# A fused layernorm, Fourier filter and MLP kernel: the program's block is taken away, and one small early read with it

## The chip, the cores and the metric

The kernel runs on one core of one Trainium2 chip. The core has five engines that run their own instruction streams: TensorE (PE in the profile; its weight loads are listed as PEld), VectorE (DVE), ScalarE (ACT), GpSimd (POOL) and SyncE (SP). SP, ACT and POOL also issue DMA transfers, each on a queue of its own. The engines wait for one another and for transfers through semaphores only. The metric is device time in microseconds (us); lower is better.

## What is computed

For an input x of 2048 rows by 640 columns (bf16) the kernel returns

```python
x = A_x
xn = _layernorm(x, axis=-1)
return x + _A_ref(xn, A_w_r, A_w_i) + _B_ref(xn, B_w1, B_b1, B_w2, B_b2)
```

`_A_ref` is a two-dimensional real FFT of xn, a product with the complex weights `w_r + 1j * w_i`, and the inverse FFT. `_B_ref` is `gelu(xn @ w1 + b1) @ w2 + b2`, with w1 of 640 by 1536 and w2 of 1536 by 640.

## The kernel before

The 2048 rows are worked on as 16 tiles of 128 rows. The transforms are products with tables (`gtab`, `etab`, `mtab`, `ntab`, `getab`, `htab`), the MLP is two matrix products with W1 and W2, and everything runs on TensorE, in bf16, out of on-chip memory.

The program is not written engine by engine. Every instruction group is registered as an operation with `K.op` (class `Sched`, line 221): the engine, what it reads and writes, and a function that emits it. Operations are numbered in the order of registration. `ORDER` (line 158) gives, by these numbers, the order of the work on each engine. `Sched.schedule` (line 260) walks through that order with planned times, and hands out buffers (PSUM banks among them) by these times; `LAND` and `LATE` (lines 191 and 192) correct the planned landing of single transfers. `Sched.sync` (line 373) finds which semaphore waits are needed. `Sched.emit` (line 417) writes the five instruction streams.

In `emit`, `nc.Block()` is entered at line 428 (the profile puts the instructions of its end at line 493, where the surrounding `with` stands), and the function `run` writes each engine's stream inside the block at lines 444 to 448. Inside a block, each engine's stream is a body of its own: the engine branches from the program's common start into its body, and at the end of the body it branches to the block's end, where it executes a DRAIN and all five engines meet: four of them raise a semaphore, POOL waits for all four and then releases them. SP's stream ends with waits for the 18 stores of the output (lines 440 to 442). A similar meeting of all engines stands ahead of the block; it belongs to the program's constructor (line 989) and not to the block.

The start, as far as it matters here:

- SP issues, in the order of `ORDER["sp"]`, the first tile of x (operation 8), the second tile (14), W1's first chunk (15), tiles 2 and 3 of x (18), and W1's other four chunks (16, 17, 20, 19). W1 is cut by rows into five chunks of 128 rows, 384 KB each.
- ACT issues two small reads, `wtouch` (operation 12, lines 606 and 607) and b1 (13, line 608), and then loads its table for the gelu (operation 9, line 601).
- `wtouch` reads 16 pieces of 256 bytes, one from every eighth row of W1's first chunk, into a tile that nothing uses. Its buffer `B_touch` is named among the things that the b1 matmul (line 659) reads, so that matmul waits for it.
- PE runs 38 matmuls on zeros (`warm`), then transposes the first normalised tiles (line 718), runs the b1 matmul (line 659), and starts on the first MLP product, chunk by chunk of W1 (lines 767 to 777). Nearly all matmuls of the program have the line 552 in the profile, as they are emitted by one helper.

At the end, the last tile's output is made in three pieces (line 958: 320, 160 and 160 columns); each goes through a DVE addition (line 961) and a store issued by SP (line 964).

Of the kernel before, what the change touches and what calls it, by code (L numbers as in the profile page):

```python
# [14 lines left out]
F = 1536  # L15
# [3 lines left out]
NFC = 12  # L19
# [104 lines left out]
class Pool:  # L124
# [31 lines left out]


ORDER = {
    "sp": """8 14 15 18 16 17 20 19 22 23 21 28 31 24 27 29 154 156 167 169 33 32 36 47 49 38 180 182 193 195 39 40 42 35 45 34
30 53 50 41 206 220 222 208 44 43 51 46 52 48 37 55 509 507 506 508 530 532 531 533 555 554 54 556 557 579 578 581  # L160
580 600 645 609 626 636 672 662 681 744 698 753 735 718 769 708 778 785 792""",
    "pe": """7 118 56 120 279 261 123 234 252 243 125 270 235 271 244 253 262 282 255 237 236 280 254 264 273 246 265 274 238
# [9 lines left out]
780 767 773 781 774 782 775 776 783 786 787 788 789 790""",  # L172
    "act": """12 13 9 119 57 124 140 259 143 277 260 278 268 251 269 250 293 320 241 242 296 136 314 135 137 323 317 311 308 152
# [3 lines left out]
577 467 461 464 745 455 449 452 761 458 585 736 770 673 612 648 647 683 684 720 756""",  # L177
    "dve": """0 59 58 60 62 63 64 116 117 122 121 67 66 126 68 71 70 138 72 128 127 141 129 131 132 130 145 144 75 77 74 78 76 79
# [6 lines left out]
725 755 743 697 758 734 752 757 759 760 717 768 707 777 784 791""",  # L185
    "pool": """10 11 3 1 2 61 5 65 6 69 73 80 87 94 4 101 108 26 115 25 592 690 618 628 654 710 664 700 727 746 638 602 762 737
771 674""",
}


LAND = {8: 3.13, 14: 3.63, 15: 5.7, 16: 8.08, 17: 9.04, 19: 11.01, 20: 10.03, 21: 14.89, 22: 11.84, 23: 12.65, 24: 17.41, 27: 18.61, 28: 15.54, 29: 19.46, 31: 16.42}
LATE = {18: 0.5, 25: 0.4, 26: 0.7, 30: 2.0, 32: 1.0, 34: 0.5, 35: 1.6, 36: 1.4, 38: 1.4, 39: 0.4, 40: 1.7, 41: 2.3, 42: 1.7, 43: 0.2, 44: 0.4, 45: 2.5, 46: 0.4, 47: 2.2, 48: 0.9, 49: 1.6, 50: 2.9, 51: 0.3, 52: 1.2, 53: 2.5, 156: 0.3, 169: 0.9, 180: 1.0, 182: 1.0, 193: 0.6, 206: 1.0, 220: 0.7, 592: 1.1}


class Op:
# [25 lines left out]
class Sched:  # L221
# [195 lines left out]
    def emit(self, es, last):  # L417
        nc = self.nc
        sems = {e: nc.alloc_semaphore(f"s_{e}") for e in self.engines if e != "sp"}
        for e in self.engines:  # L420
            n = 0
            for o in self.order[e]:
                if o.nbytes:
                    o.sem, o.count = nc.alloc_semaphore(f"d_{o.seq}"), 16
                elif o.inc:
                    n += 1
                    o.sem, o.count = sems[e], n
        block = es.enter_context(nc.Block())

        def run(name):  # L430
            def go(e):
                for o in self.order[name]:
                    for d in o.waits:
                        e.wait_ge(d.sem, d.count)
                    ins = o.emit(e, name) if o.alts is None else o.emit(e, o.alt)
                    if o.nbytes:
                        ins.then_inc(o.sem, 16)
                    elif o.inc:
                        ins.then_inc(o.sem, 1)
                if name == "sp":  # L440
                    for o in last:
                        e.wait_ge(o.sem, o.count)
            return go
        block.sync(run("sp"))
        block.gpsimd(run("pool"))
        block.vector(run("dve"))
        block.scalar(run("act"))
        block.tensor(run("pe"))


BLOCKS = [(0, 2), (2, 2), (4, 2), (6, 2), (8, 4), (12, 4)]
# [19 lines left out]
def bass_parallel_sum__spectral_gfnet__dense_activation_gelu__prompt_kernel(  # L471
# [15 lines left out]
    w1v = B_w1.rearrange("(c p) f -> p c f", p=128)  # L487
# [5 lines left out]
    with ExitStack() as es:  # L493
        def sb(name, shape, dtype=BF):
            return es.enter_context(nc.sbuf_tensor(name, shape, dtype))
# [9 lines left out]
        ident = sb("ident", [128, 128])  # L505
# [5 lines left out]
        getab = sb("getab", [128, 800])  # L511
        htab = sb("htab", [128, 16, 128])
        b1t = sb("b1t", [NFC, 128])
        wtouch = sb("wtouch", [16, 128])
        b1col = sb("b1col", [128, NFC], F32)
        b2bc = sb("b2bc", [128, D])
        stats = sb("stats", [128, 16, 15], F32)
# [21 lines left out]
        def psb(slot, dims, off=0, p0=0, n=128):  # L539
            return bass.AP(tensor=PS, offset=p0 * 4096 + slot * 512 + off, ap=[[4096, n]] + dims)  # L540
# [5 lines left out]
        def load(dst, src, buf, rows, after=(), q="sp", issue=0.46, prio=400, gate=(), late=0.0):  # L546
            return K.op([(q, 0.7 if q == "pool" else issue)], prio, lambda e, _: e.dma_start(dst, src), writes=[buf], after=after, rows=rows, gate=gate, late=late)
# [8 lines left out]
        def pe(segs, prio, lst, **kw):  # L556

            return K.op([("pe", sum(u for _, u in segs))], prio, mms(lst), alts=[segs], **kw)
# [24 lines left out]
        B_id, B_b1, B_b2b = Buf("ident"), Buf("b1t"), Buf("b2")  # L583
# [14 lines left out]
        def load_w1(j, q="sp"):  # L598
# [4 lines left out]
        K.op([("pool", 0.3)], 410, lambda e, _: e.memset(ident[:], 1.0), writes=[B_one])  # L603
        K.op([("pool", 0.5)], 410, lambda e, _: e.affine_select(out=ident[:], in_=ident[:], pattern=[[-1, 128]], compare_op=ALU.is_equal, fill=0.0, base=0, channel_multiplier=1),
             reads=[B_one], writes=[B_id])
        B_touch = Buf("touch")
        load(wtouch[:], bass.AP(tensor=w1v.tensor, offset=w1v.offset, ap=[[8 * F, 16], [1, 128]]), B_touch, (1, 256), q="act", prio=406)
        load(b1t[:], b1v, B_b1, (1, 256), q="act", prio=405)
        load_x(1, 1)
        load_w1(0)  # L610
# [45 lines left out]
        load(htab[:].rearrange("p a b -> p (a b)"), const["H"], B_h, (8, 4096), gate=turned[5])  # L656

        B_b1ps, B_b1c = Buf("b1ps", psum), Buf("b1col")
        pe([("128", 0.1)], 200, lambda: [(psb(B_b1ps.slot, [[1, NFC]]), b1t[:], ident[0:NFC, 0:NFC], True, True)], reads=[B_b1, B_id, B_touch], writes=[B_b1ps])
        K.op([("act", 0.2)], 200, lambda e, _: e.activation(b1col[:], psb(B_b1ps.slot, [[1, NFC]]), ACT.Copy), reads=[B_b1ps], writes=[B_b1c])  # L660

        B_xnT = [Buf(f"xnT{c}") for c in range(16)]
# [5 lines left out]
        for c0, n in [(c, 1) for c in range(4)] + [(c, 2) for c in range(4, 16, 2)]:  # L668
            pr = 100 - c0 / 2
            B_mv, B_r = Buf(f"mv{c0}"), Buf(f"r{c0}")  # L670
            for c in range(c0, c0 + n):
                B_st = Buf(f"st{c}")
                for h in range(2):
                    st_op[c] = K.op([("dve", 0.393)], pr, lambda e, _, c=c, h=h: e.bn_stats(stats[:, c, 6 * h:6 * h + 6], view(X, c * D + H2 * h, [[1, H2]])),  # L674
                         reads=[B_x[c]], writes=[B_st], gate=mv_ops[:1])
# [3 lines left out]
                 reads=[B_mv, B_mh], writes=[B_r] + B_rs[a:b])  # L679

        for pair in range(8):
# [10 lines left out]
            for n in range(2):  # L692
# [5 lines left out]
                for d0, d1, bx in zip(cuts, cuts[1:], B_xs):  # L698
                    o = K.op([("dve", 0.066 + (d1 - d0) / 1980.0)], pr, lambda e, _, c=c, n=n, xnv=xnv, d0=d0, d1=d1: e.tensor_scalar(  # L699
                        out=xnv(n, d0, [[1, d1 - d0]]), in0=view(X, c * D + d0, [[1, d1 - d0]]), scalar1=mv[:, c, 0:1], scalar2=rstd[:, c:c + 1], op0=ALU.subtract, op1=ALU.mult),  # L700
                        reads=[B_x[c], B_rs[c]], writes=[xn, bx])
# [3 lines left out]
                if c in BYDMA:  # L705
                    ring_ops.append(K.op([("sp", 1.3)], 500, lambda e, _, c=c, n=n, xnv=xnv: e.dma_start_transpose(xnT[:, c, :, :], xnv(n, 0, [[1, D]])),
                         reads=[B_xn, xn], writes=[B_xnT[c]], rows=(40, 256)))
# [4 lines left out]
                for j0, j1, engs in ((0, 2, ["act"]), (2, 5, ["dve"])) if c < 2 else ((0, 5, ["dve", "act"]),):  # L712
# [8 lines left out]
                    if not c + j0:  # L721
# [5 lines left out]
                         reads=[tps], writes=[B_xnL[c][j0] if c < 2 else B_xnT[c]])  # L727
# [4 lines left out]
            for k, op in enumerate((ALU.add, ALU.subtract)):  # L732
                for o_, o0, o1, w in ((128 * k, 0, H2 - 1, 128), (512 + 32 * k, 128, H2 - 129, 32)):
                    ring_ops.append(K.op([("dve", dve_us(4 * w, 2))], pr, lambda e, _, op=op, x1v=x1v, xfv=xfv, o_=o_, o0=o0, o1=o1, w=w: e.tensor_tensor(  # L734
                        out=xfv(o_, [[D, 2], [2 * w, 2], [1, w]]), in0=x1v(o0, [[D, 2], [H2, 2], [1, w]]), in1=x1v(o1, [[D, 2], [H2, 2], [-1, w]]), op=op),
                        reads=[x1], writes=[xf]))
            aps = Buf(f"aps{pair}", psum, 3, ZONE["aps"])
            for n in range(2):
# [3 lines left out]
                    reads=[xf, B_g], writes=[aps])  # L742
                ring_ops.append(o)
                a_ops.append(o)
            for js in [[int(j) for j in g] for g in XASPLIT[pair].split()]:
# [3 lines left out]
                     reads=[aps], writes=[B_xa[pair]])  # L749
# [3 lines left out]
        for bi, (c0, nt) in enumerate(BLOCKS):  # L753
            for fc in range(NFC):
# [12 lines left out]
                else:  # L767
# [12 lines left out]
                    reads=[hps, B_b1c], writes=[bg])  # L780
# [223 lines left out]
```

## Time and profile before

| | |
|---|---|
| median of 3 runs | 147.75 us (147.56 to 147.98) |
| the profiled execution, its own time | 148.03 us |
| its span, from the first to the last instruction shown | 146.1 us |
| granted TensorE clock | 1.00 |
| PE busy | 140.2 us, 96% of the span |
| DVE, ACT, POOL busy | 112.7, 80.9 and 23.7 us |
| share of the chain that ended last | PE 91%, DVE 4%, issue 2%, DMA 2% |

Times in the profile are microseconds from the start of the span; the profiled execution's own time is 1.93 us longer than the span. A row of the timeline gives start, duration, engine, line, operation, what is written from what, a count, and in brackets the idle time of the engine before it with what ended it. In the view of one line, durations are in nanoseconds (least, median, greatest), followed by the first and the last start. A "q" behind an engine's name marks its sequencer: instructions that wait, branch, drain or issue a transfer, during which the engine itself counts as idle.

### The profile page before, as it was taken

To read this page: it belongs to the slowest core of one execution; us is meant where nothing else is said; L and a number is where in the kernel's file an instruction comes from. 1 tells how busy PE (TensorE), PEld (TensorE's weight loads), DVE (VectorE), ACT (ScalarE), POOL (GpSimd) and SP (SyncE) were. 2 spreads that over 40 slices of the span, in tenths; PEclk is the share of its full clock that TensorE was granted. 3 is DMA by queue.
4 is the path that set the end of the run, shared out by engine and by line. 5 is a ranking of instruction groups with operands and counts; after the bars stand their busy time and mean duration, and the time that the engine had idled before them with its cause. 6 is when DMAs were issued, how large, how long until landed. Compare 5 with 4: busy or idle time off the path is not lost.

```text
span 146.1 us, 4081 instructions
## 1 busy us (share of the span) xinstructions
PE 140.2 (96%) x1702; PEld 90.8 (62%) x1720; DVE 112.7 (77%) x235; ACT 80.9 (55%) x145; POOL 23.7 (16%) x40
## 2 busy tenths in 40 slices
PE   7999999999999999999999999999999999999993
PEld 7788998888465455446544645554446666556572
DVE  1999999999844449789966967992422998998982
ACT  3208999999989769763555633216376755201000
POOL 2330302206100009220100120000063700000000
PEclk9999999999999999999999999999999999999999
DMA  4999999999997875949446571444559885103234
GB/s 110 320 407 354 320 132 303 150 182 241 283 162 149 193 192 123 235 99 180 94 92 121 63 154 30 40 110 94 90 116 230 175 202 180 45 4 137 90 135 135
DMA packets 30873, 23.63 MB, mean 162 GB/s; under 512 B 20488, under 2 KB 26888, under 8 KB 30728
## 3 DMA queue, kind: packets, MB, share of 16 engines
q1 hardware_dynamic: 28432, 17.81, 52.4%
q0 software_dynamic: 2368, 5.57, 17.4%
q8 instruction: 13, 0.21, 0.6%
q14 instruction: 4, 0.03, 0.1%
q10 hardware_dynamic: 56, 0.01, 0.0%
HBM read 13.55 MB, written 2.62 MB: 111 GB/s over the span
## 4 chain that ended last, share of the span: by engine, by line
PE 91%; DVE 4%; issue 2%; DMA 2%; POOL 0%
PE ps L552 90%; DVE stats L674 2%; DMA X<-in_A_x_dram 2%; DVE T L699 1%; DVE mv L676 0%; DVE xnT L564 0%; POOL rstd L678 0%; PE ps L718 0%; DVE W L961 0%
## 5 line engine op out<-in xcount | busy, mean ns | idle before, releaser
L552 PE MATMUL ps<-xnT,W 128*128 128x256 bf16 (+2 forms) x384 | 58.7, 300 | 0.2 <-DVE mv L676 0.2
L552 PE MATMUL ps<-W,gT 128*128 128x512 bf16 (+3 forms) x380 | 55.7, 292 | 1.6 <-issue 1.1
L552 PEld LDWEIGHTS ps<-W,gT 128*128 128x128 bf16 x396 | 30.3, 98 | 23.5 <-issue 1.6
L552 PEld LDWEIGHTS ps<-xnT,W 128*128 128x128 bf16 x384 | 33.3, 98 | 16.3 <-issue 1.6
L778 ACT ACTIVATE gT<-ps,b1col 128x256 bf16<-128x256 f32 (+1 forms) x72 | 35.3, 557 | 6.8 <-PE ps L552 6.5
L674 DVE BATCH_NORM_STATS2 stats<-X 128x6 f32<-128x320 bf16 x32 | 13.9, 475 | 2.2 <-DMA X<-in_A_x_dram 2.2
L563 ACT ACTIVATE Wf<-ps 128x960 bf16<-128x960 f32 (+1 forms) x8 | 7.0, 901 | 13.5 <-PE ps L552 13.5
L946 POOL DMA_DIRECT2D X<-in_A_x_dram x8 | 7.1, 1067 | 40.1 <-DMA Wf<-in_A_w_r_dram 17.6
L845 DVE TENSOR_TENSOR T<-Y,Wf 128x1288 bf16<-128x1288 bf16 x16 | 12.7, 826 | 0.0
L946 POOL DMA_DIRECT2D xnT<-in_A_x_dram x8 | 7.4, 1151 | 25.3 <-ACT xnT L928 25.3
L678 POOL TENSOR_TENSOR rstd<-mv,mhalf 128x2 f32<-128x2 f32 (+1 forms) x10 | 7.2, 715 | 26.8 <-DVE mv L676 26.7
L563 ACT ACTIVATE Xb<-ps 128x960 bf16<-128x960 f32 (+1 forms) x7 | 7.7, 1102 | 6.8 <-PE ps L552 6.8
L564 DVE CAST Y<-ps 128x644 bf16<-128x644 f32 x8 | 6.5, 828 | 5.5 <-PE ps L552 5.5
L563 ACT ACTIVATE XV<-ps 128x1280 bf16<-128x1280 f32 (+3 forms) x10 | 9.5, 961 | 0.7 <-PE ps L552 0.7
L564 DVE CAST Xb<-ps 128x960 bf16<-128x960 f32 (+1 forms) x5 | 5.9, 1176 | 4.1 <-PE ps L552 4.1
L734 DVE TENSOR_TENSOR T<-T 128x512 bf16<-128x512 bf16 (+1 forms) x32 | 8.5, 311 | 0.0
L699 DVE TENSOR_SCALAR T<-X,mv,rstd 128x640 bf16<-128x640 bf16 (+2 forms) x17 | 7.1, 430 | 0.9 <-POOL rstd L678 0.6
L900 DVE TENSOR_TENSOR Wf<-Wf 128x960 bf16<-128x960 bf16 (+1 forms) x12 | 7.0, 597 | 0.5 <-ACT Wf L563 0.3
L961 DVE TENSOR_TENSOR W<-ps,X 128x640 bf16<-128x640 f32 x8 | 6.5, 820 | 1.1 <-PE ps L552 1.1
L849 DVE TENSOR_TENSOR Z<-T 128x644 bf16<-128x644 bf16 x16 | 7.1, 487 | 0.1
L961 DVE TENSOR_TENSOR W<-ps,xnT 128x640 bf16<-128x640 f32 (+2 forms) x10 | 6.7, 685 | 0.7 <-PE ps L552 0.7
L552 PE MATMUL ps<-etab,XV 32*128 32x160 bf16 (+1 forms) x128 | 7.2, 232 | 0.0
(55 smaller groups left out, 132.3 us busy)
## 6 DMA issues: line engine op xcount, KB each, us to landing
X<-in_A_x_dram POOLq DMA_DIRECT2D x8, 320.0 KB, 4.8
xnT<-in_A_x_dram POOLq DMA_DIRECT2D x8, 320.0 KB, 5.0
out_dram<-W SPq DMA_DIRECT2D x15, 160.0 KB, 1.8
X<-in_A_x_dram SPq DMA_DIRECT2D x7, 320.0 KB, 7.5
W<-in_B_w_dram SPq DMA_DIRECT2D x5, 384.0 KB, 6.1
W<-in_B_w_dram SPq DMA_DIRECT2D x4, 480.0 KB, 7.5
Wf<-in_A_w_i_dram SPq DMA_DIRECT2D x6, 160.5 KB, 5.8
Wf<-in_A_w_r_dram SPq DMA_DIRECT2D x6, 160.5 KB, 4.1
```

The source lines that it names most:

```text
L552: ins = e.matmul(o_, lhsT=lw, rhs=rh, start=st, stop=sp_, skip_group_check=True)
L563: return e.activation(dst(), src(), ACT.Copy, scale=scale)
L564: return e.tensor_copy(dst(), src())
L674: st_op[c] = K.op([("dve", 0.393)], pr, lambda e, _, c=c, h=h: e.bn_stats(stats[:, c, 6 * h:6 * h + 6], view(X, c * D + H2 * h, [[1, H2]]) ...
L678: K.op([("pool", 0.65)], 500, lambda e, _, a=a, b=b: e.tensor_tensor(out=rstd[:, a:b], in0=mv[:, a:b, 1], in1=mhalf[:, a:b], op=ALU.pow), ...
L699: o = K.op([("dve", 0.066 + (d1 - d0) / 1980.0)], pr, lambda e, _, c=c, n=n, xnv=xnv, d0=d0, d1=d1: e.tensor_scalar(out=xnv(n, d0, [[1, d1 ...
L734: ring_ops.append(K.op([("dve", dve_us(4 * w, 2))], pr, lambda e, _, op=op, x1v=x1v, xfv=xfv, o_=o_, o0=o0, o1=o1, w=w: e.tensor_tensor(ou ...
L778: K.op([("act", act_us(128 * nt, 1))], pr + PRIO["gelu"] + GP[bi], lambda e, _, c0=c0, nt=nt, fc=fc, hps=hps, at=at: e.activation(gT[:, fc ...
L845: filt_ops.append(K.op([("dve", dve_us(4 * KP, 2))], pr, lambda e, _, k=k, Y=Y, TB=TB, pair=pair: e.tensor_tensor(out=view(TT, TB.slot * 8 ...
L849: K.op([("dve", dve_us(2 * KP, 2))], pr, lambda e, _, TB=TB, Z=Z, r=r, op=op: e.tensor_tensor(out=view(Zb, Z.slot * 4 * KP + r * KP, [[2 * ...
L946: xo_ops[c] = K.op([("pool", 0.9)], 51 - c / 20, lambda e, _, c=c, xov=xov: e.dma_start(xov(0, D), xv[:, c, :], accum_op=ALU.add), reads=[ ...
L961: K.op([("dve", dve_us(w))], 95, lambda e, _, os_=os_, fps=fps, o0=o0, w=w, xov=xov, base=base: e.tensor_tensor(out=view(W1, OST + os_.slo ...
```

## The change

The block is taken away: the five streams are written directly, one after the other, through the engines' handles. The small read `wtouch` is taken away with its tile, its buffer and its place among the b1 matmul's inputs. As operations are numbered in order, every number above 12 falls by one in `ORDER`, `LAND` and `LATE`; apart from the missing operation 12 the five orders are the same. One planned landing differs: that of W1's first chunk, 5.7 before and 5.8 after.

```diff
...
-    "act": """12 13 9 119 57 124 140 259 143 277 260 278 268 251 269 250 293 320 241 242 296 136 314 135 137 323 317 311 308 152
...
+    "act": """12 9 118 56 123 139 258 142 276 259 277 267 250 268 249 292 319 240 241 295 135 313 134 136 322 316 310 307 151 298
...
-LAND = {8: 3.13, 14: 3.63, 15: 5.7, 16: 8.08, 17: 9.04, 19: 11.01, 20: 10.03, 21: 14.89, 22: 11.84, 23: 12.65, 24: 17.41, 27: 18.61, 28: 15.54, 29: 19.46, 31: 16.42}
...
+LAND = {8: 3.13, 13: 3.63, 14: 5.8, 15: 8.08, 16: 9.04, 18: 11.01, 19: 10.03, 20: 14.89, 21: 11.84, 22: 12.65, 23: 17.41, 26: 18.61, 27: 15.54, 28: 19.46, 30: 16.42}
...
-        block = es.enter_context(nc.Block())
...
-        block.sync(run("sp"))
-        block.gpsimd(run("pool"))
-        block.vector(run("dve"))
-        block.scalar(run("act"))
-        block.tensor(run("pe"))
+        run("sp")(nc.sync)
+        run("pool")(nc.gpsimd)
+        run("dve")(nc.vector)
+        run("act")(nc.scalar)
+        run("pe")(nc.tensor)
...
-        wtouch = sb("wtouch", [16, 128])
...
-        B_touch = Buf("touch")
-        load(wtouch[:], bass.AP(tensor=w1v.tensor, offset=w1v.offset, ap=[[8 * F, 16], [1, 128]]), B_touch, (1, 256), q="act", prio=406)
...
-        pe([("128", 0.1)], 200, lambda: [(psb(B_b1ps.slot, [[1, NFC]]), b1t[:], ident[0:NFC, 0:NFC], True, True)], reads=[B_b1, B_id, B_touch], writes=[B_b1ps])
+        pe([("128", 0.1)], 200, lambda: [(psb(B_b1ps.slot, [[1, NFC]]), b1t[:], ident[0:NFC, 0:NFC], True, True)], reads=[B_b1, B_id], writes=[B_b1ps])
...
```

More of the change, by code (lines that the diff above doesn't have):

```diff
@@ L158 @@
 ORDER = {
[L159 to L162, printed above, removed]
[9 rows of a table removed]
-780 767 773 781 774 782 775 776 783 786 787 788 789 790""",
-    "act": """12 13 9 119 57 124 140 259 143 277 260 278 268 251 269 250 293 320 241 242 296 136 314 135 137 323 317 311 308 152
[3 rows of a table removed]
@@ L177 @@
-577 467 461 464 745 455 449 452 761 458 585 736 770 673 612 648 647 683 684 720 756""",
-    "dve": """0 59 58 60 62 63 64 116 117 122 121 67 66 126 68 71 70 138 72 128 127 141 129 131 132 130 145 144 75 77 74 78 76 79
[6 rows of a table removed]
-725 755 743 697 758 734 752 757 759 760 717 768 707 777 784 791""",
-    "pool": """10 11 3 1 2 61 5 65 6 69 73 80 87 94 4 101 108 26 115 25 592 690 618 628 654 710 664 700 727 746 638 602 762 737
-771 674""",
-}
-LAND = {8: 3.13, 14: 3.63, 15: 5.7, 16: 8.08, 17: 9.04, 19: 11.01, 20: 10.03, 21: 14.89, 22: 11.84, 23: 12.65, 24: 17.41, 27: 18.61, 28: 15.54, 29: 19.46, 31: 16.42}
@@ L192 @@
-LATE = {18: 0.5, 25: 0.4, 26: 0.7, 30: 2.0, 32: 1.0, 34: 0.5, 35: 1.6, 36: 1.4, 38: 1.4, 39: 0.4, 40: 1.7, 41: 2.3, 42: 1.7, 43: 0.2, 44: 0.4, 45: 2.5, 46: 0.4, 47: 2.2, 48: 0.9, 49: 1.6, 50: 2.9, 51: 0.3, 52: 1.2, 53: 2.5, 156: 0.3, 169: 0.9, 180: 1.0, 182: 1.0, 193: 0.6, 206: 1.0, 220: 0.7, 592: 1.1}
+    "sp": """8 13 14 17 15 16 19 18 21 22 20 27 30 23 26 28 153 155 166 168 32 31 35 46 48 37 179 181 192 194 38 39 41 34 44 33
+29 52 49 40 205 219 221 207 43 42 50 45 51 47 36 54 508 506 505 507 529 531 530 532 554 553 53 555 556 578 577 580
@@ new lines @@
+579 599 644 608 625 635 671 661 680 743 697 752 734 717 768 707 777 784 791""",
+    "pe": """7 117 55 119 278 260 122 233 251 242 124 269 234 270 243 252 261 281 254 236 235 279 253 263 272 245 264 273 237
[9 rows of a table added]
+779 766 772 780 773 781 774 775 782 785 786 787 788 789""",
+    "act": """12 9 118 56 123 139 258 142 276 259 277 267 250 268 249 292 319 240 241 295 135 313 134 136 322 316 310 307 151 298
[3 rows of a table added]
+466 460 463 744 454 448 451 760 457 584 735 769 672 611 647 646 682 683 719 755""",
+    "dve": """0 58 57 59 61 62 63 115 116 121 120 66 65 125 67 70 69 137 71 127 126 140 128 130 131 129 144 143 74 76 73 77 75 78
[6 rows of a table added]
@@ new lines @@
+724 754 742 696 757 733 751 756 758 759 716 767 706 776 783 790""",
+    "pool": """10 11 3 1 2 60 5 64 6 68 72 79 86 93 4 100 107 25 114 24 591 689 617 627 653 709 663 699 726 745 637 601 761 736
+770 673""",
+}
+LAND = {8: 3.13, 13: 3.63, 14: 5.8, 15: 8.08, 16: 9.04, 18: 11.01, 19: 10.03, 20: 14.89, 21: 11.84, 22: 12.65, 23: 17.41, 26: 18.61, 27: 15.54, 28: 19.46, 30: 16.42}
+LATE = {17: 0.5, 24: 0.4, 25: 0.7, 29: 2.0, 31: 1.0, 33: 0.5, 34: 1.6, 35: 1.4, 37: 1.4, 38: 0.4, 39: 1.7, 40: 2.3, 41: 1.7, 42: 0.2, 43: 0.4, 44: 2.5, 45: 0.4, 46: 2.2, 47: 0.9, 48: 1.6, 49: 2.9, 50: 0.3, 51: 1.2, 52: 2.5, 155: 0.3, 168: 0.9, 179: 1.0, 181: 1.0, 192: 0.6, 205: 1.0, 219: 0.7, 591: 1.1}
```

36 rows, old and new, of the table ORDER are left out of this document.

## The prediction

> **What bounds the kernel now.** I read the stretches first: the middle must be known before the two ends are worth anything.
>
> ```profile
> 13.00:143.50 130.50, 128.70 (x1577) 80.78 (x1592) 102.78 (x205) 77.19 (x139) 20.29 (x25) 1.00 0.70 149
> 143.50:146.10 2.60, 0.05 (x1) 0.00 (x0) 0.32 (x1) 0.00 (x0) 0.00 (x0) 1.00 0.34 102
> ```
>
> The columns are the length of the stretch, then busy time and instructions of PE, PEld, DVE, ACT and POOL, the granted clock, the DMA share and GB/s. From 13 us to 143.5 us PE works 128.70 of 130.50 us at the full clock. There is nothing to lose a delay in: what PE starts later at 13 us, it ends later by nearly as much, and what it starts earlier it gains. Everything that the change touches lies before 13 us or behind the last matmul, so the question is what is on the path at these two ends.
>
> At the front end, I take the issues of W1's five chunks on SP, one window each (the last figure is the time from issue to landing), and PE's rows at the place where they are used:
>
> ```profile
> 0.81 0.87 SPq L547 DMA_DIRECT2D X<-in_A_x_dram  x2
> 1.73 0.43 SPq L547 DMA_DIRECT2D W<-in_B_w_dram  x1
> 2.67 1.96 SPq L547 DMA_DIRECT2D W<-in_B_w_dram  x4
> ...
> W<-in_B_w_dram SPq DMA_DIRECT2D x1, 384.0 KB, 4.0
> ...
> W<-in_B_w_dram SPq DMA_DIRECT2D x1, 384.0 KB, 6.1
> ...
> W<-in_B_w_dram SPq DMA_DIRECT2D x1, 384.0 KB, 7.1
> ...
> 6.44 0.40 PE L552 MATMUL ps<-xnT,W 128*128 128x128 bf16 x4
> 7.29 1.88 PE L552 MATMUL ps<-xnT,W 128*128 128x128 bf16 x30
> 7.62 0.34 DVE L564 COPY xnT<-ps 128x384 bf16<-128x384 bf16 x1
> 9.38 1.29 PE L552 MATMUL ps<-xnT,W 128*128 128x256 bf16 x10 [0.21 <-DVE mv L676]
> ```
>
> The first chunk, issued at 1.73, lands at 5.7; PE first needs it at 6.44, so it has 0.7 us to spare. The third is the second of the four issues from 2.67 on (1.96 / 4 = 0.49 us apart, so about 3.16) and lands 6.1 later, at about 9.26. The last is issued at about 4.14 and lands 7.1 later, at about 11.2. At 9.38 the profile names a DVE instruction as what ended PE's 0.21 us of waiting. But the DVE result that this matmul reads is the copy that ended at 7.62 + 0.34 = 7.96, so it was the third chunk's landing. PE is thus paced by W1's chunks until about 11.2 us: a chunk that lands later by some time moves all that follows by that time. That makes the small read of W1 worth a look, small as it is.
>
> At the back end:
>
> ```profile
> 143.58 0.32 DVE L961 TENSOR_TENSOR W<-ps,xnT 128x160 bf16<-128x160 f32 x1 [0.24 <-PE ps L552]
> ...
> L964 SPq DMA_DIRECT2D out_dram<-W x18: 332/334/453, 120.1 to 144.0; - x18
> ...
> L442 SPq EVENT_SEMAPHORE  x9: 17/28/28, 144.5 to 145.6; - x9
> ...
> L493 POOLq EVENT_SEMAPHORE  x2: 17/17/17, 145.9 to 145.9; - x2
> L493 POOLq DRAIN  x1: 6442/6442/6442, 115.2 to 115.2; - x1
> L493 ACTq DRAIN  x1: 732/732/732, 134.0 to 134.0; - x1
> L493 PEldq DRAIN  x1: 1702/1702/1702, 141.9 to 141.9; - x1
> L493 DVEq DRAIN  x1: 361/361/361, 143.6 to 143.6; - x1
> L493 SPq COMPARE_BRANCH  x1: 41/41/41, 145.7 to 145.7; - x1
> L493 SPq DRAIN  x1: 7/7/7, 145.8 to 145.8; - x1
> L493 SPq EVENT_SEMAPHORE  x1: 17/17/17, 146.0 to 146.0; - x1
> ...
> L493 PEldq EVENT_SEMAPHORE  x1: 51/51/51, 146.0 to 146.0; - x1
> ```
>
> These are the instructions of the block's end (line 493) and the waits for the stores (line 442). The last store is issued at 144.0; the last of the nine wait instructions starts at 145.6; then come SP's branch at 145.7, its drain at 145.8, POOL's two steps at 145.9, and the release of the others at 146.0, where the span ends. POOL's drain is the long one, 6.4 us, but it ends at 121.6, under PE's work. All engines but SP are through their drains by 144.0, so they wait for SP, and the block's end stands on the path from 145.7 to 146.1 with nothing beside it.
>
> **The change part by part.**
>
> *The block's end.* Removed are five branches, five drains and the meeting. SP's branch carries the last of its waits; that wait stays, as one more wait instruction of up to 28 ns behind the one at 145.6, so SP ends near 145.7 in place of 146.1. The rows are given to a tenth: the gain lies between 0.30 and 0.45 us. I take 0.37.
>
> *The block's start.* Five branches into the bodies. The chain of waits begins:
>
> ```profile
> 0.74 0.07 issue
> 0.81 2.34 DMA X<-in_A_x_dram
> ...
> 9.34 0.04 issue
> ```
>
> From the release of the first meeting to the first issue pass 0.07 us, and the branch is somewhere in it. An issue step elsewhere in the same chain is 0.02 to 0.04 us, so the branch has 0 to 0.07 us; I take 0.05, nearer to the upper end, as SP's branch at the end took 41 ns. This stands on the path: both x and W1 are issued behind it.
>
> *The time around the span.* The profiled execution took 148.03 us, 1.93 us over the span. The trace shows nothing of what is in it. Without the meeting, four engines are done before SP: PE at 141.9 + 1.7 = 143.6, DVE at 144.0, ACT and POOL long before. What they have to do at the program's end can then be done under SP's waits. From below that is nothing, if only SP's own steps count; from above it is all 1.93 us. The only row for an engine's delay behind the release is PE's 51 ns against SP's 17 ns. I take 0.05 us, close to the lower end, as that row is. The Trainium skill ("Runtime: NRT & Kernel Launch", section "The launch sequence") says that a barrier of all engines follows the kernel, at about 1.5 us. By it this term is zero, as SP would be awaited there in any case, and the sum would be 0.42 instead of 0.47; no run here shows that stretch.
>
> *The small read: what leaves with it.* One issue on ACT, one wait on PE, and 16 pieces of 256 bytes.
>
> ```profile
> 0.81 0.42 ACTq L547 DMA_DIRECT2D wtouch<-in_B_w_dram  x1
> ...
> 1.26 0.64 ACTq L547 DMA_DIRECT2D b1t<-in_B_b_dram  x1
> ...
> 1.93 1.28 ACT L601 ACT_TABLE_LOAD   x1 [1.93 <-issue]
> ...
> 5.57 0.39 PE L718 MATMUL ps<-ident,T 128*128 128x128 bf16 x2 [0.28 <-DVE T L699]
> 5.89 0.10 PEld L552 LDWEIGHTS ps<-ident,b1t 12*128 12x128 bf16 x1 [0.20 <-issue]
> 6.00 0.38 ACT L563 ACTIVATE xnT<-ps 128x256 bf16<-128x256 bf16 x1 [2.79 <-PE ps L718]
> ```
>
> ACT's b1 read and table load start about 0.45 us earlier (1.26 to 0.81). ACT is idle for 2.79 us before it is first needed at 6.00, so this is worth nothing; if that cover were gone it would be worth those 0.45 us. PE's wait stood ahead of the b1 matmul at 5.89, under a stretch in which the next real work at 6.44 waits for ACT's copy of 6.00 to 6.38: nothing. The pieces themselves are 4 KB beside the 384 KB of one chunk: at the 414 GB/s of the row below, 0.01 us.
>
> *The small read: what it may have done for W1.* It touched W1's first chunk before the chunk's own load. If that made the first contact cheaper, the load will now be slower.
>
> ```profile
> 1.75:3.00 1.25, 1.25 (x15) 1.25 (x13) 0.00 (x0) 1.07 (x1) 0.00 (x0) 1.00 0.79 239
> 3.00:3.50 0.50, 0.50 (x8) 0.50 (x6) 0.33 (x1) 0.21 (x1) 0.00 (x0) 1.00 1.07 176
> 3.50:4.00 0.50, 0.50 (x7) 0.50 (x6) 0.50 (x2) 0.00 (x0) 0.00 (x0) 1.00 0.69 129
> 4.00:4.50 0.50, 0.50 (x8) 0.50 (x6) 0.47 (x3) 0.00 (x0) 0.10 (x1) 1.00 0.75 251
> ...
> 8.00:11.00 3.00, 2.79 (x38) 2.39 (x36) 2.96 (x10) 0.02 (x1) 1.22 (x2) 1.00 1.03 414
> ```
>
> Between 3.0 and 4.5, when W1's first chunk begins to move, the queues deliver 0.5 x (176 + 129 + 251) = 278 KB. At 414 GB/s it would be 621 KB. So 0.83 us is lost there, with the small read in place. The first contact with x, from 1.75 on, had no small read ahead of it and still ran at 239 GB/s, queue start included. So the rows show no good that the read does, and they show a stall it did not prevent. I take 0. From above: were half of the stall already paid by the small read, its removal would cost another 0.83 us. From below: were the read itself part of the trouble, up to 0.83 us could come back, but PE can use only what it waits at the chunks, the 0.21 us at 9.38 and, as an estimate, no more than that again at the two chunks behind it, so 0.4 us.
>
> *The plan.* The landing planned for W1's first chunk moves by 0.1 us, and one ACT operation less is planned. The orders are equal otherwise, but PSUM banks are handed out by planned times, so a bank and with it a wait can change. The nearest row is PE's 0.21 us at 9.38: up to 0.2 us either way, once. I take 0, as PE's work and order are the same.
>
> *Sum.* 0.37 + 0.05 + 0.05 + 0 + 0 = 0.47 us: 148.03 becomes 147.56 for an execution like the profiled one. That execution lies 0.28 us above the median of the runs, so I forecast 147.75 - 0.47 = 147.28 us.
>
> **The rivals.** A change under 0.3%, 0.44 us here (147.31 to 148.19), is about what a measurement of this kernel cannot tell from none; the forecast lies at that border.
>
> - *The end saves more than the span shows.* A good part of the 1.93 us outside the span is work of engines that are now early. For: they are early by 1.7 us or more against the end of the wait at 145.7 (PE 2.1, DVE 1.7). Against: SP's own end is still last. With a third of it, 0.65 us in place of 0.05: 147.28 - 0.60 = 146.7 us.
> - *W1 lands later by part of a stall.* For: the stall of 0.83 us sits where the read aimed. Against: the read did not prevent it. With half of it, 0.4 us: 147.7 us, no change that can be told; with all of it 148.1.
> - *Slower: W1's first contact is paid in full.* If the read had prepaid two thirds of the first contact, its removal costs twice the visible stall, 1.66 us: chunk one lands at 7.4 instead of 5.7, eats its 0.7 us of room, and the chunks behind it on SP's queue come as late, so PE runs 1.66 us late from 8 us on. 147.28 + 1.66 = 148.9 us. It decides from 0.91 us on, that is when the last chunk lands after 12.1. Against: chunks two to five had no small read and the 414 GB/s of 8 to 11 us leave no stall.
> - *The change doesn't do what it says.* The meeting is removed from the span, and the time around the span grows by as much, because the engines meet there anyway. Then only the start is gained: 147.7 us.
>
> **How the numbers follow.** The forecast 0.38 (with the uncertain terms 147.05 to 147.5; about 0.27 of it under 147.31 and 0.11 above); the end saving more 0.20; W1 later by a part 0.25; slower 0.12; nothing saved 0.05. Faster: 0.27 + 0.20 = 0.47. Within: 0.11 + 0.25 + 0.05 = 0.41. Slower: 0.12. The range reaches from 146.6, a little past the rival at the end, to 148.0, nearly all of the stall; outside it are the slower case and the tails of the two rivals. The forecast's own range is 147.05 to 147.5.
>
> **What would show it.** At the end: no instruction of line 493 apart from any that the program's end puts there, SP's last wait as the last row, and a span shorter by 0.4 us behind the same last store. At the start: the first issue of x earlier than 0.81, at 0.76. Around the span: its own time less its span, against 1.93 us: a clear fall speaks for the first rival, a rise for the last. W1: the landing of the first chunk (5.7) and, what counts, of the third and the last (9.26, 11.2) and the GB/s from 3.0 to 4.5: unchanged by my forecast. The sum is wrong if PE's start on the third chunk, 9.38, moves by more than 0.2 us either way, and its reasoning is wrong if PE's 1.8 us of idle time between 13 and 143.5 us change by more than that.

## The result, and the profile after

The changed kernel takes 146.65 us in the median of 8 runs (146.26 to 147.38), against 147.97 us for the kernel before beside it. The ratio is 0.9916 with a 95% interval of 0.9892 to 0.9940: faster, by 0.8%, some 1.2 us. In a later set of runs, beside the last experiments, the ratio was 0.9903 (0.9872 to 0.9934).

The profiled execution of the changed kernel took 147.25 us with a span of 146.0 us. That is a span hardly shorter than the 146.1 us of before. So the first thing to look at is not a row of the trace but the difference between an execution's own time and its span, which every run lists (the row of before is from the runs beside the first experiments, as no spans are known of those beside this result; spans are given to a tenth of a microsecond):

| | own time less span, median (least to most) | span, median (least to most) |
|---|---|---|
| before, 34 runs | 1.94 us (1.85 to 2.11) | 145.8 us (145.4 to 147.4) |
| changed, 8 runs | 1.28 us (1.21 to 1.30) | 145.35 us (145.0 to 146.1) |

About 0.7 us of the gain lies outside what the trace shows: 0.66 us by this table, and 0.77 us in the last set, where both kernels ran side by side (2.03 against 1.26 us). Inside the span the medians differ by 0.25 to 0.45 us (145.8 and 145.35 here, 145.9 and 145.5 in the last set, 145.8 and 145.55 for the kernel below that gives up the block alone). Spans of one kernel spread over one to two microseconds, times outside the span by 0.1 to 0.3; the first column of figures is by far the sharper tool here.

Inside the span, these are the waits for the stores and the stores themselves in the changed kernel (the view of one line: durations in ns, then the first and last start in us), and under them the answer for line 493:

```profile
L960 SPq DMA_DIRECT2D out_dram<-W x18: 332/334/456, 120.4 to 144.3; - x18
...
L441 SPq EVENT_SEMAPHORE  x9: 28/28/28, 144.8 to 145.9; - x9
...
nothing on L493; most used: ['L550', 'L433', 'L774', 'L561', 'L545', 'L714', 'L562', 'L670', 'L730', 'L957', 'L960', 'L985', 'L695', 'L672', 'L726', 'L924', 'L841', 'L942', 'L845', 'L866', 'L702', 'L896', 'L901', 'L674', 'L948']
```

The block's end is gone entirely. The last wait starts at 145.9 and the span ends at 146.0, where before the last of the nine waits started at 145.6 and the span ended at 146.1. From the last store's issue to the span's end pass 1.7 us (144.3 to 146.0), where before it was 2.1 (144.0 to 146.1): the rows show a saving of 0.4 us. The last store is issued 0.3 us later than before, and that hides the saving in this one execution.

At the front end, the timeline of the first microseconds, PE's row behind its first wait for W1, and W1's chunks (the DMA view of one issue each, the first, third and last chunk; the last figure is from issue to landing):

```profile
0.80 0.61 ACTq L545 DMA_DIRECT2D b1t<-in_B_b_dram  x1
...
0.81 0.88 SPq L545 DMA_DIRECT2D X<-in_A_x_dram  x2
...
1.45 1.28 ACT L599 ACT_TABLE_LOAD   x1 [1.45 <-PEq L985]
1.73 0.43 SPq L545 DMA_DIRECT2D W<-in_B_w_dram  x1
...
8.18 2.38 PE L550 MATMUL ps<-xnT,W 128*128 128x128 bf16 x28 [0.25 <-DMA W<-in_B_w_dram]
...
W<-in_B_w_dram SPq DMA_DIRECT2D x1, 384.0 KB, 4.1
W<-in_B_w_dram SPq DMA_DIRECT2D x1, 384.0 KB, 6.0
W<-in_B_w_dram SPq DMA_DIRECT2D x1, 384.0 KB, 7.0
```

ACT's b1 read and table load start earlier by 0.46 and 0.48 us, as the prediction had it, and x and W1 are issued at the same 0.81 and 1.73 as before. The chunks take 4.1, 6.0 and 7.0 us to land, against 4.0, 6.1 and 7.1. The second chunk, which the prediction passed over, took 5.5 against 5.3, and PE waited 0.25 us for it at 8.18. Over all profiles its landing took 4.6 to 6.2 us without the small read and 5.2 and 5.3 with it, and PE waited for it in five of the eleven profiles without the read and in neither of the two with it; whether the read has a part in that is not shown, and the times below show no loss by it. By the chains of waits PE is no later for it at the last chunk: at 12.26 us here, at 12.36 before. The stretches show the slow start of W1 once more (the columns are those of the prediction; the last is GB/s):

```profile
3.00:3.50 0.50, 0.50 (x8) 0.50 (x7) 0.48 (x2) 0.00 (x0) 0.00 (x0) 1.00 1.23 211
3.50:4.00 0.50, 0.50 (x7) 0.50 (x6) 0.47 (x3) 0.00 (x0) 0.00 (x0) 1.00 0.58 199
4.00:4.50 0.50, 0.50 (x10) 0.50 (x8) 0.50 (x3) 0.00 (x0) 0.25 (x1) 1.00 1.03 334
```

They move 0.5 x (211 + 199 + 334) = 372 KB between 3.0 and 4.5 us, against 278 KB before. At 414 GB/s it would again be 621 KB, so 0.6 us is lost in place of 0.83: the stall is there without the small read too, and it is not worse.

Between the ends, PE's work is the same. The two programs differ on each engine only by the block's branches, drains and meeting, by the small read on ACT, by one wait on PE, and by how SP's waits for the stores are paired: the nine wait instructions now hold all 18, and the one that stood on the branch needed no instruction more. The tensors behind `wtouch` lie 256 bytes lower in on-chip memory; no bank of PSUM and no buffer within a tensor moved with the planned landing of 5.8 us. The stretch from 13 to 143.5 us looks different all the same:

```profile
13.00:143.50 130.50, 130.24 (x1591) 80.41 (x1589) 102.99 (x206) 77.31 (x139) 20.43 (x25) 1.00 0.69 149
```

PE idles for 0.26 us in it, where the profile of before showed 1.80. That is no gain. The trace of before holds 1702 matmuls beside 1720 weight loads, every other trace 1720 of both, and the 18 that are missing belong where its chain of waits has 18 gaps of 0.05 or 0.16 us on PE, 1.8 us together. Such a row of gaps stands in no other profile; with the block and without the read, PE works 130.16 of the 130.50 us. PE was thus even closer to full than the prediction read.

The chain of waits tells where the profiled execution lost its 0.3 us:

```profile
21.93 7.80 DMA X<-in_A_x_dram
...
35.63 108.28 PE ps L550 x1359
```

The load of tiles 14 and 15 of x took 7.8 us to land, where in the profiled execution of before it took 4.8. It stands on the chain up to 29.7, and the DVE work behind it makes PE wait 0.26 us at 35.6. This doesn't go with the block: the load took 6.8 us in the block's kernel without the small read, below, and 4.8 in one of the kernels without the block; in the other profiles it took 7.0 to 7.9.

### The profile page after: what moved, and what is told of

Same layout as the page of the kernel before. It is cut to its first block, busy times and chain, and to the rows that moved or that the text cites. A ratio compares the mean times of both kernels' runs of the same rounds, so it can differ in the third digit from the quotient of the medians.

```text
span 146.0 us, 4085 instructions
## 1 busy us (share of the span) xinstructions
PE 141.7 (97%) x1720; PEld 90.3 (62%) x1720; DVE 112.6 (77%) x235; ACT 81.1 (56%) x145; POOL 23.8 (16%) x40
## 4 chain that ended last, share of the span: by engine, by line
PE 80%; DMA 9%; DVE 6%; SPq 2%; issue 1%; POOL 1%
PE ps L550 80%; DMA X<-in_A_x_dram 5%; DMA W<-in_B_w_dram 4%; DVE T L730 2%; SPq L545 2%; DVE T L726 1%; DVE stats L670 1%; POOL rstd L674 1%; PE ps L714 0%; DVE mv L672 0%; SPq L702 0%; DVE T L695 0%; DVE W L957 0%
## 5 line engine op out<-in xcount | busy, mean ns | idle before, releaser
L550 PE MATMUL ps<-W,gT 128*128 128x512 bf16 (+3 forms) x396 | 58.7, 295 | 0.0
```

Of the source, the lines that this page charges most:

```text
L550: ins = e.matmul(o_, lhsT=lw, rhs=rh, start=st, stop=sp_, skip_group_check=True)
```

## The experiments

**Which part of the change gains.** Two kernels do one half of the change each. The first takes away the block and keeps the small read:

```diff
-        block = es.enter_context(nc.Block())
...
-        block.sync(run("sp"))
...
-        block.tensor(run("pe"))
+        run("sp")(nc.sync)
...
+        run("pe")(nc.tensor)
```

> The block is gone, the small read of W1 stays. Theory 1 (the whole gain is the block's, the read does nothing): time like the changed kernel's, 146.3 to 147.0 us, ratio to before about 0.991; own time less span about 1.28 us. Rival (part of the gain is the read's): at least 0.3 us slower than the changed kernel, ratio 0.994 or more. Rival the other way (the read helps and its loss was covered by the block's gain): ratio 0.989 or less.

Measured: 146.78 us, ratio 0.9929 (0.9903 to 0.9956); own time less span 1.25 us. The time outside the span is the changed kernel's; the ratio lies between the first two cases, and its interval reaches both. The second keeps the block and leaves the small read out, with the changed kernel's orders:

```diff
...
-        wtouch = sb("wtouch", [16, 128])
...
-        load(wtouch[:], bass.AP(tensor=w1v.tensor, offset=w1v.offset, ap=[[8 * F, 16], [1, 128]]), B_touch, (1, 256), q="act", prio=406)
...
```

> The block stays, the small read is gone. Theory 1: no change against before, ratio 0.998 to 1.002, own time less span about 1.93 us, W1's first chunk landing within 0.2 us of 5.7. If the read is a brake: ratio 0.997 or less. If it helps: 1.003 or more.

Measured: 147.90 us, ratio 1.0011 (0.9988 to 1.0035); own time less span 1.96 us. So the gain is the block's, and the read's share is nothing that can be told from zero: taken away alone, between a gain of 0.12% and a loss of 0.35%. W1's first chunk landed at 5.8 us with the read and without the block, 5.7 without the read and with the block.

**What lies outside the span.** Two theories were left. A: at a program's end each engine has something to do that the trace does not show, and without the meeting four engines do it while SP still waits for the stores. B: the block's own code costs it, by its branches or by one more fetch of instructions. To tell them apart, the four engines are made late again without any block:

```diff
                 if name == "sp":
                     for o in last:
                         e.wait_ge(o.sem, o.count)
+                if name in ('pool', 'dve', 'act', 'pe'):
+                    e.wait_ge(last[-1].sem, last[-1].count)
```

> The changed kernel, with PE, DVE, ACT and POOL each waiting at their end for the last store, as SP does: nobody is early, but there is no meeting and no branch. Theory A (the 0.65 us outside the span are work that the four engines do at the program's end, which is now done under SP's waits): own time less span goes back to about 1.9 us, time about 147.2. Theory B (they come from the block's code itself, its branches or one more fetch of instructions behind the end): own time less span stays at 1.28 us, time like the changed kernel's.

Measured: own time less span 1.92 us (1.87 to 1.95, 10 runs), time 147.45 us, ratio 0.9982 (0.9945 to 1.0019). The view of the two lines shows the waits:

```profile
L441 SPq EVENT_SEMAPHORE  x9: 28/28/28, 144.6 to 145.8; - x9
L443 ACTq EVENT_SEMAPHORE  x1: 17/17/17, 145.8 to 145.8; - x1
L443 POOLq EVENT_SEMAPHORE  x1: 17/17/17, 145.8 to 145.8; - x1
L443 DVEq EVENT_SEMAPHORE  x1: 21/21/21, 145.8 to 145.8; - x1
L443 PEldq EVENT_SEMAPHORE  x1: 51/51/51, 145.8 to 145.8; - x1
```

Nothing was added that takes time in the span: each engine's extra wait takes 17 to 51 ns and begins with SP's last one, at 145.8, where the span ends. Yet nearly all of the 0.66 us came back, and the time, expected at 147.2, came back by as much: this kernel and the one that only gives up the block, run in the same set, have the same median span, 145.55 us, and 147.45 against 146.78 us in all. Theory A holds, and B falls as the cause of the 0.66 us: there is no branch in this program. Its other test puts the meeting back without the block's branches:

```diff
         run("pe")(nc.tensor)
+        nc.all_engine_barrier()
```

> The changed kernel with the drains and the meeting of all engines put at its end, without the branches of a block. Theory A: own time less span about 1.9 us, time as before the change or 0.1 us less, 147.6 to 147.9. Theory B: own time less span 1.28 us, and only the 0.4 us of the meeting in the span come back, 147.0.

Measured: own time less span 1.98 us, time 147.56 us, ratio 0.9994 (0.9967 to 1.0021), no more to be told from before. The meeting alone, then, undoes the change. It does so outside the span; the median span is 145.55 us here too, so that medians of the span are too coarse to show the meeting's own rows. These are:

```profile
L441 SPq EVENT_SEMAPHORE  x9: 28/28/28, 145.4 to 146.5; - x9
L448 POOLq EVENT_SEMAPHORE  x2: 17/17/17, 146.6 to 146.7; - x2
L448 POOLq DRAIN  x1: 7552/7552/7552, 116.1 to 116.1; - x1
...
L448 SPq DRAIN  x1: 7/7/7, 146.6 to 146.6; - x1
...
L448 PEldq EVENT_SEMAPHORE  x1: 51/51/51, 146.7 to 146.7; - x1
```

From the last wait's start (146.5) to the span's end (146.8) it takes 0.3 us; with the block's branch in between it was 0.5 (145.6 to 146.1). SP's branch at the block's end is thus worth 0.1 to 0.2 us of the 0.4 in the span, by one profile each. The profile's own 41 ns for it is only part of what it costs.

**Which engine.** The same wait, given to one engine at a time:

```diff
+                if name in ('pe',):
+                    e.wait_ge(last[-1].sem, last[-1].count)
```

> The changed kernel, PE alone waits for the last store as SP does. Theory A1 (one engine's work at the program's end takes 0.65 us longer than SP's): own time less span 1.9 us if PE is that engine, 1.28 if not. Theory A2 (the engines end one after the other, each adds a share): about 1.28 + 0.65 / 4 = 1.44 us for each engine.

> The same with ACT alone. A1: 1.9 us if it is ACT, else 1.28. A2: about 1.44.

> The same with DVE alone. A1: 1.9 us if it is DVE, else 1.28. A2: about 1.44.

> The same with POOL alone. A1: 1.9 us if it is POOL, else 1.28. A2: about 1.44.

| who ends with the last store | own time less span, median | runs |
|---|---|---|
| SP alone (the changed kernel) | 1.28 us | 8 |
| SP and DVE | 1.36 us | 2 |
| SP and ACT | 1.43 us | 9 |
| SP and PE | 1.56 us | 2 |
| SP and POOL | 1.92 us | 8 |
| SP and all four | 1.92 us | 10 |

Neither form was right as written. It isn't one engine against equal others, and the shares don't add up: DVE, ACT, PE and POOL together would add 0.08 + 0.15 + 0.28 + 0.64 = 1.15 us to 1.28, and all four gave 1.92, which is POOL's alone. So for each engine a time of its own length passes from its last instruction to the program's end, these times run side by side, and the one that is over last sets the time. What passes in it, work of the engine itself or its place in a common closing, the trace doesn't show. The figures for PE and DVE here rest on two runs each. The ratios of these kernels, 0.9893 (0.9763 to 1.0022) with PE, 0.9902 (0.9869 to 0.9934) with ACT, 0.9873 (0.9743 to 1.0003) with DVE and 0.9942 (0.9900 to 0.9984) with POOL, are too wide to show it; the times outside the span do.

If that is so, an engine may be late by as much as its end is shorter than the longest, and POOL must be early by 1.92 - 1.28 = 0.64 us. This was put to the test with POOL waiting for the last store but one:

```diff
+                if name == "pool":
+                    e.wait_ge(last[-2].sem, last[-2].count)
```

> The changed kernel, POOL alone waits at its end for the last store but one, which lands about 0.5 us before the last. Theory A1, in its sharper form (each engine has a fixed end of its own, POOL's 1.93 us, SP's 1.28, and the latest of them sets the time): own time less span 1.93 - 0.48 = 1.45 us. Rival (POOL's end is long whenever POOL still waits on anything at that point): 1.9 us.

```profile
L441 SPq EVENT_SEMAPHORE  x9: 27/28/28, 144.2 to 145.3; - x9
L443 POOLq EVENT_SEMAPHORE  x1: 17/17/17, 144.9 to 144.9; - x1
```

Measured: 1.46 us (1.42 to 1.50, 8 runs), where 1.45 was expected, and the rival's 1.9 falls. POOL's wait is over at 144.9, SP's last at 145.3; what POOL's end sticks out beyond SP's is what is paid. This kernel and the one in which POOL waits for the last store have the same instructions and differ only in which store is waited for, so their 1.92 and 1.46 us can't come from the code or its fetching.

One remainder stays open. In the kernel before, POOL's last step starts at 145.9, about 0.1 us ahead of the span's end; with ends of fixed length that would leave 1.8 us outside the span. Measured are 1.94 us in the first set and 2.03 in the two later ones, and 1.98 with the meeting put back. The latest end thus accounts for all but 0.1 to 0.2 us, and what the meeting adds beyond it isn't shown.

**Can another engine be last more cheaply?** DVE waits for the stores, and SP ends with its last issue:

```diff
-                if name == "sp":
+                if name == "dve":
                     for o in last:
                         e.wait_ge(o.sem, o.count)
```

> The changed kernel, but DVE instead of SP waits for the 18 stores; SP ends with its last issue. Latest-end form of theory A: own time less span 1.36 us, as with DVE and SP both waiting, so 0.1 us slower than the changed kernel. If the ends run one after the other with SP's share in them: less than 1.28 us, and faster than the changed kernel.

Measured: 1.36 us outside the span (1.31 to 1.39, 10 runs), time 146.83 us, ratio 0.9920 (0.9892 to 0.9948). The time outside is DVE's own, as the latest-end form has it, with SP early. By the times outside the span, SP is the engine that can be last most cheaply, as it is in the changed kernel, and neither this version nor the others above beat it. The closing run of the changed kernel beside these:

> The changed kernel once more, for a closer interval: ratio to before 0.991 to 0.994; own time less span 1.28 us.

Measured: 146.81 us, ratio 0.9903 (0.9872 to 0.9934), 1.26 us outside the span. The ratio came out a little under the expected 0.991, well inside its interval.

## Why the prediction was right or wrong

The direction and the range held: 147.28 us was forecast, 146.6 to 148.0 as the range, and 146.65 was measured. The range held by 0.05 us, less than the runs can tell (the interval of the ratio reaches down to 146.4), so that is luck in part. The forecast's own range, 147.05 to 147.5, was missed, and its gain of 0.47 us was well under half of the measured one. Point by point:

- *The block's end, 0.37 us: right.* All rows of line 493 are gone, and the span ends with SP's last wait. From the last store's issue to the span's end the rows are 0.4 us shorter. The medians of the spans fell by 0.25 to 0.45 us, too coarse to say more. The one more wait instruction that the prediction counted wasn't needed.
- *The block's start, 0.05 us: wrong, it is nothing.* The first issue of x stands at 0.81 in both profiles. The 0.07 us of issue ahead of it is still there in the chain, without a branch in it. The estimate leaned on the 41 ns of the other branch; the lower bound, 0, was the right end.
- *The time around the span, 0.05 us: the term that was mis-sized.* It measured 0.66 to 0.77 us. The prediction saw the place (four engines early by 1.7 us and more) and both bounds, 0 and 1.93, and then took the lower end, by PE's 51 ns, a row of another thing: how late an engine leaves the meeting says nothing on what it does behind it. The rival "the end saves more than the span shows" put it at 0.65 us, 146.7 us in all, with a chance of 0.20. It had the mechanism; its size, a third of 1.93 us, was worked out from no row, so that it fits so well is luck. Its "against" (SP's own end is still last) was the wrong question: what counts is whose end is longest, and that is POOL's by 0.64 us. The prediction also set the Trainium skill's rule on the launch sequence ("Runtime: NRT & Kernel Launch", section "The launch sequence") beside this term, and concluded that it would be zero. The runs disagree with that conclusion: the time after the last instruction was not one fixed length behind the last engine, but 1.28 to 1.92 us depending on which engine was last.
- *What bounds the kernel: right, by a reading that was not.* The prediction called its reasoning wrong if PE's 1.8 us of idle time in the middle changed by more than 0.2, and the profile after shows 0.26 us. The 1.8 us were matmuls that the trace of before lacks, so the sign came up without the reasoning being wrong: a PE that idles for 0.26 us has even less room to make up a delay.
- *The small read, 0: right.* Off ACT it moved b1 and the table load forward by nearly half a microsecond, under cover, for nothing. For W1's first, third and last chunk it did nothing that shows (the second varies, as said above), and the stall it stood in front of was there with and without it. The rivals that rested on it (a part or all of a stall) fell. "Paid in full" would have had the last chunk land after 12.1 us; it landed at 11.1.
- *The plan, 0: right.* No bank of PSUM and no buffer within a tensor moved.
- *"The change doesn't do what it says": fell,* with the opposite sign: the time around the span shrank instead of growing.

The profiled execution alone would have misled: its span fell by 0.1 us, as a load of x landed late in it (7.8 us), which doesn't go with the change.

## What to carry to other kernels

Compare an execution's own time with its span before reading rows: a change at a program's end can gain or lose outside everything that the trace shows. If engines needn't meet at the end, let them finish on their own and have the one with the shortest end (here SP) wait for the stores; the engine with the longest (here POOL, 0.64 us longer than SP's) must be done that much before. An early read meant to smooth a later load is worth keeping only if its removal shows.

## What the runs showed of the hardware that was not expected

- From an engine's last instruction to the program's end passes a time that depends on the engine: 1.28 us on SP, 1.36 on DVE, 1.43 on ACT, 1.56 on PE (two runs) and 1.92 on POOL, and these times run in parallel. For DVE it was the same 1.36 with SP early and with SP late.
- The taken branch at the block's end cost 0.1 to 0.2 us on SP, where its row says 41 ns; the branch at the block's start cost nothing that the rows show (first issue at 0.81 us with and without it).
- While W1's first chunk lands, between 3.0 and 4.5 us, the queues moved 278 KB with the small read and 372 KB without it, where 414 GB/s would have moved 621 KB. What causes it stays open.
- Spans of one kernel differ by one to two microseconds between executions (145.4 to 147.4 us before, 145.0 to 146.1 changed); one load of x took from 4.8 to 7.9 us to land.
- A trace can lack matmuls: 18 of 1720 in the profile of before, which looked like 1.8 us of idle time.
